# Three-stage chain on one core: the sign of each converted weight as a signed float zero made on GpSimd, the joins a step later, and 26 subtractions moved to GpSimd

## The chip, the cores and the metric

One core of a Trainium2 chip runs the whole program. The metric is the device time of one execution in microseconds (us), lower is better. The engines are called by their names and by the short names of the profile: TensorE (PE, its weight loads PEld), VectorE (DVE), ScalarE (ACT), GpSimd (POOL) and SyncE (SP), whose queue issues nearly all of the transfers.

## The reference

The inputs are of double width in memory where they are weights. What is computed, cut to what matters:

```python
def _attn_ref(q, k, v, tau):            # B, N, C = 2, 6016, 256
    qn = q / (norm(q, axis=1) + 1e-06); kn = k / (norm(k, axis=1) + 1e-06)
    s = kn.transpose(0, 2, 1) @ qn / tau        # 256 x 256 for each batch
    a = softmax(s)
    return v @ a

def _moe_ref(x, w_in, w_out):           # 12032 x 256, 256 x 2048, 2048 x 256
    h = x @ w_in
    return (h - tanh(h)) @ w_out

def _moe2_ref(x, w_gate, w_val, w_out): # 256 x 1536 twice, 1536 x 256
    return (sigmoid(x @ w_gate) * (x @ w_val)) @ w_out
```

The weights `w_in`, `w_out`, `w_gate`, `w_val` and the second `w_out` are stored as 64-bit floats, so the kernel reads each of them as two 32-bit words.

## The kernel before, in words

The columns of `v` (12032 over both batches) are cut into 24 blocks of 496 or 512. Every block goes through `h` (2048 rows, 16 pieces `f` of 128), the elementwise part of the first stage (`emit_E`), `x` (`emit_X`), then the gate and the value (`emit_GV`, 12 pieces), and the output (`emit_O`). The attention matrix of a batch is multiplied into `w_in` once (`aw_chunk`, eight chunks), so that `h` comes straight out of `v`. Nearly every matmul is done in three parts: a number is split into a high part in the fast 32-bit format (a ScalarE copy, `hi`) and a low part (a VectorE subtraction, `lo`), and high times high, high times low and low times high are summed.

The order is written out by hand: a loop over steps `T`, from -4 on, emits for each step, in this order on every engine: the two elementwise halves of the piece whose `h` was computed one step before, the splits for `x` and the output, the gate and value matmuls of the step, the `h` matmuls (ahead of the rest in the first 16 steps), a chunk of `aw` in the even steps up to 12, the `x` matmuls of two steps before, and then the background work. Background work is a list of generators (`running`, filled by `at(step, fn)`): each advances by one `yield` in a step, the older ones first, and those of the same step start after them. An engine runs its instructions in that order and none other.

The weights are converted in the first 250 us, in `conv` (L117 to L150). A generator of `conv` loads a tile of raw words `st` (512 KB, SP's queue), then in the next step ScalarE makes `bt` from the high words (a scaled copy, L135) and a second scaled copy as a half float in place of the high words' upper halves (L136), VectorE puts three bits of the low word beside it (L138) and joins both into the 32-bit float (L143). For the weights of the last two products one more step makes `hi` on ScalarE (L149) and `lo` on VectorE (L150). In the background list `whole` runs a generator, passing over each `yield 1`. In `tail`, in the softmax of the first batch, every `yield` counts, and a list written by hand places them. There are 34 conversions: eight of `w_in` (`conv_win`), eight of the first `w_out` (`conv_w1`, into `w1_f`, split later by `split_w1`, L184 and L187) and 18 of the second stage (`conv_m2`).

The raw tiles of the last 28 of them come from the pool `v4`, which has three buffers and also holds the loaded blocks of `v` (`load_v`) and the output tiles. Between step 4, where block 1 of `v` is loaded, and step 16, where it is split, one of the three is taken. `conv_w1` of chunk 2 to 7 starts at the steps 3, 5, ... 13, and `conv_m2` at 4, 6, ... 14 and then by a formula that keeps it ahead of `GV0`, the steps of the first block's gate matmuls.

GpSimd does a few memsets at the start, and from step 54 on one sum of squares every second step (L688, `acc`). PSUM has four buffers for `h`, `aw`, gate and value.

Of the kernel before, what the change touches and what calls it, by code (L numbers as in the profile page):

```python
# [8 lines left out]
F32 = mybir.dt.float32  # L9
F32R = mybir.dt.float32r  # L10
BF16 = mybir.dt.bfloat16
U32 = mybir.dt.uint32
U16 = mybir.dt.uint16
F16 = mybir.dt.float16
AF = mybir.ActivationFunctionType
ALU = mybir.AluOpType
AX = mybir.AxisListType

P = 128
# [8 lines left out]
def kernel(  # L28
# [13 lines left out]
    nc = tc.nc  # L42
# [18 lines left out]
    rest, i = N - WB * nb, nb // 2  # L61
    assert 0 <= rest <= nb * (TB - WB)
    while rest:
        widths[i] += QB
        rest -= QB
        i = (i + 1) % nb
    blocks = []
    for b in range(B):
        t = 0
# [6 lines left out]
    const = ctx.enter_context(tc.tile_pool(name="const", bufs=1))  # L76
# [16 lines left out]
    def cv(name, shape=(P, 512)):  # L93
        return cv_p.tile(list(shape), F32, tag="cv", name=name)
# [4 lines left out]
    def psw(name, shape=(P, 512)):  # L99
        return ps_w.tile(list(shape), F32, tag="w", name=name)  # L100

    ones = const.tile([P, P], F32, name="ones")
    nc.vector.memset(ones, 1.0)
    ident = const.tile([P, P], F32, name="ident")
# [12 lines left out]
    w1_hi = [wp.tile([P, 2, C], F32R, name=f"w1h{i}") for i in range(N1 // 2)]  # L117
    w1_lo = {}
    win_d = dr_p.tile([N1 // 2, P, NK, 2 * P], F32, name="win_d")

    def conv(src, shape, pool, tag, name, w=None, hi=None, lo=None):

        a, m = shape
        st = pool.tile([P, a, 2 * m], U32, tag=tag, name=f"st_{name}")
        nc.sync.dma_start(out=st, in_=src)
        yield
        words = st.rearrange("p a (m t) -> p a m t", t=2)
        low, high = words[:, :, :, 0], words[:, :, :, 1]
        half = st.bitcast(U16).rearrange("p a (m t) -> p a m t", t=4)
        bt = cv(f"cb_{name}", (P, a, m))  # L130
        bu = bt.bitcast(U32)

        nc.scalar.activation(bt, high.bitcast(F32), AF.Copy, scale=2.0**-112)  # L135
        nc.scalar.activation(half[:, :, :, 3].bitcast(F16), high.bitcast(F32), AF.Copy, scale=2.0**-96)  # L136
        yield 1
        nc.vector.tensor_scalar(half[:, :, :, 2], half[:, :, :, 1], 13, None, ALU.logical_shift_right)  # L138
        yield 1
        yield 1  # L140
        if callable(w):
            w = w()
        nc.vector.scalar_tensor_tensor(  # L143
            out=bu if w is None else w.bitcast(U32), in0=bu, scalar=3, in1=high,
            op0=ALU.logical_shift_left, op1=ALU.bitwise_or
        )
        if w is None:
            yield
            nc.scalar.activation(hi, bt, AF.Copy)  # L149
            nc.vector.tensor_tensor(out=lo, in0=bt, in1=hi.bitcast(F32), op=ALU.subtract)  # L150

    def whole(g):

        for x in g:
            if x is None:
                yield

    def words(ap):
        return ap.bitcast(U32)

    def conv_win(i, pool, tag="st"):
        src = words(w_in)[:, i * 512:(i + 1) * 512].rearrange("(k p) f -> p k f", p=P)
        yield from conv(src, (NK, 2 * P), pool, tag, f"wi{i}", w=win[i])
# [7 lines left out]
    w1_f = {}  # L171

    def conv_w1(i):
        src = words(w_out)[i * 256:(i + 1) * 256, :].rearrange("(a p) d -> p a d", p=P)

        def home():
            pool, tag = (wp, f"w1l{i - 4}") if i > 3 else (wp2, f"w2{'hl'[i % 2]}{4 + i // 2}")
            w1_f[i] = pool.tile([P, 2, C], F32, tag=tag, name=f"w1f{i}")
            return w1_f[i]

        return conv(src, (2, C), v4_p, "v4", f"w1{i}", w=home)

    def split_w1(i):
        nc.scalar.activation(w1_hi[i], w1_f[i], AF.Copy)  # L184
        yield
        w1_lo[i] = wp.tile([P, 2, C], F32R, tag=f"w1l{i}", name=f"w1l{i}")
        nc.vector.tensor_tensor(out=w1_lo[i], in0=w1_f[i], in1=w1_hi[i].bitcast(F32), op=ALU.subtract)  # L187


    kq = {}  # L190
# [291 lines left out]
    while len(e_of) < NT:  # L482
        for home in ("x2h", "x2l", *(f"rr{i}" for i in range(6))):
            j = len(e_of)
            n = min(2 if home[0] == "x" else 1, NT - j)
# [174 lines left out]
    def conv_m2(i, which):  # L660
        if which == 2:
            src = words(w_out2)[i * 256:(i + 1) * 256, :].rearrange("(a p) d -> p a d", p=P)
            for x, nm in ((w2_hi, "w2h"), (w2_lo, "w2l")):
                x[i] = wp2.tile([P, 2, 2 * P], F32R, tag=f"{nm}{i}", name=f"{nm}{i}")
            h, lo = w2_hi[i], w2_lo[i]
        else:
            w = (w_gate, w_val)[which]
            src = words(w)[:, i * 512:(i + 1) * 512].rearrange("(k p) f -> p k f", p=P)
            h, lo = ((wg_hi[i], wg_lo[i]), (wv_hi[i], wv_lo[i]))[which]
        return conv(src, (2, 2 * P), v4_p, "v4", f"m{which}{i}", hi=h, lo=lo)  # L670
# [31 lines left out]
    def at(step, fn, *a):  # L702
        bg.setdefault(step, []).append((fn, a))
# [3 lines left out]
    GV0 = (20, 21, 22, 24, 25, 27, 28, 30, 31, 33, 34, 35)  # L707
# [6 lines left out]
    for i in range(N1 // 2):  # L714
        at({6: 16, 2: 18, 7: 19, 3: 20, 4: 21, 5: 23, 0: 25, 1: 26}[i], split_w1, i)
# [4 lines left out]
            at(2 * i - 9 if i < 6 else 2 * i - 5, win_store, i)  # L720
    for n in range(3 * N2 // 2):
        i, w = divmod(n, 3)
        late = GV0[2 * i] - 3 + (w == 2)
        at(min(late, 4 + 2 * n if n < 6 else 7 + 3 * n // 2), lambda i=i, w=w: whole(conv_m2(i, w)))
    at(2 * N1 + 7, ks_load)
    for j in range(NT):
        t = 54 + 2 * j
# [121 lines left out]
```

## Time and profile before

| what | value |
|---|---|
| median of three runs | 2211.99 us (2211.82 to 2213.15) |
| the profiled execution | 2212.01 us, of which the span of the profile is 2210.2 us |
| TensorE busy | 2199.5 us of the span |
| VectorE busy | 1772.7 us |
| ScalarE busy | 1602.0 us |
| GpSimd busy | 66.5 us |
| granted TensorE clock | full in every slice |

The profile is of one execution. An engine's busy time says how much of the span it worked; the waits say what ended its idle time; the tables by stretch of time show where an engine is near its limit. A busy TensorE is not TensorE at its peak, since the ends of its matmuls are modelled. Times that lie outside the span (1.8 us here) are launch and end.

### The profile page before, as it was taken

Reading aid. Unit: us, or ns where it says so; the run is one execution under the profiler, and the core shown is the slowest. Engines: PE = TensorE matmul, PEld = TensorE weight load, DVE = VectorE, ACT = ScalarE, POOL = GpSimd, SP = SyncE. Lnnn points to the kernel's source line nnn. Section 1 sums busy time; section 2 is a strip of 40 time slices with the busy share of each in tenths; the row PEclk is TensorE's granted clock in tenths of the full one; section 3 lists DMA queues with packets and bytes.
Section 4 is the critical chain, followed back from the end, with each engine's and each line's share of the span. In section 5 each row is a group of like instructions: output and inputs, shape, how many; then the busy total and the mean of one; then the engine's idle time right before and its main releaser. Section 6 shows DMA issues by size and latency. Waiting matters only on the chain.

```text
span 2210.2 us, 28820 instructions
## 1 busy us (share of the span) xinstructions
PE 2199.5 (100%) x10338; PEld 1944.1 (88%) x10338; DVE 1772.7 (80%) x2723; ACT 1602.0 (72%) x2811; POOL 66.5 (3%) x53
## 2 busy tenths in 40 slices
PE   9999999999999999999999999999999999999999
PEld 8778899898888888888999999999988888888898
DVE  7889877888888888878787787787787877877773
ACT  7988867777777777767677676776776776767763
POOL 0000000111111110000000000000000000000000
PEclk9999999999999999999999999999999999999999
DMA  9742101111111010001000000000000000000000
GB/s 354 241 147 96 38 1 53 34 29 52 35 29 48 27 36 20 1 24 34 19 19 1 19 19 1 19 19 1 19 20 1 19 20 1 20 1 19 10 1 19
DMA packets 54000, 86.54 MB, mean 39 GB/s; under 512 B 4960, under 2 KB 31072, under 8 KB 53856
## 3 DMA queue, kind: packets, MB, share of 16 engines
q1 hardware_dynamic: 53280, 83.91, 11.6%
q8 instruction: 81, 1.33, 0.3%
q10 hardware_dynamic: 576, 0.79, 0.1%
q14 instruction: 63, 0.52, 0.1%
HBM read 69.73 MB, written 14.94 MB: 38 GB/s over the span
## 4 chain that ended last, share of the span: by engine, by line
PE 93%; DVE 3%; ACT 3%; issue 1%; DMA 1%; ACTq 0%; DVEq 0%
PE o L445 16%; PE h L332 14%; PE h L334 7%; PE x L381 7%; PE x L378 7%; PE x L379 7%; PE va L414 5%; PE va L416 5%; PE va L413 5%; PE ga L414 5%; PE ga L413 5%; PE ga L416 5%; PE x L373 2%; PE kqe L517 1%; PE aw L285 1%
## 5 line engine op out<-in xcount | busy, mean ns | idle before, releaser
L347 DVE SCALAR_TENSOR_TENSOR w<-u,h 128x496 f32<-128x496 f32 (+1 forms) x384 | 259.6, 676 | 228.6 <-ACT t L343 227.7
L350 DVE COPY_PREDICATED w<-m,t 128x496 f32<-128x496 uint16 (+1 forms) x384 | 303.9, 792 | 39.9 <-ACT sr L687 0.5
L342 ACT ACTIVATE u<-h 128x496 f32<-128x496 f32 (+1 forms) x384 | 222.7, 580 | 138.8 <-PE h L334 138.3
L345 ACT ACTIVATE s<-u,cb 128x496 f32<-128x496 f32 (+1 forms) x384 | 273.8, 713 | 0.3 <-DVE w L349 0.3
L346 ACT ACTIVATE m<-u,ct 128x496 bf16<-128x496 f32 (+1 forms) x384 | 272.5, 710 | 0.0
L348 DVE TENSOR_TENSOR t<-h,t 128x496 f32<-128x496 f32 (+1 forms) x384 | 258.4, 673 | 0.0
L349 DVE SCALAR_TENSOR_TENSOR w<-s,w 128x496 f32<-128x496 f32 (+1 forms) x384 | 257.6, 671 | 0.0
L332 PE MATMUL h<-vTh,awh 128*128 128x496 f32 (+1 forms) x768 | 232.8, 385 | 0.0
L334 PE MATMUL h<-vTh,awl 128*128 128x496 f32 (+1 forms) x768 | 225.1, 375 | 0.2 <-DVE awl L291 0.2
L332 PE MATMUL h<-vTl,awh 128*128 128x496 f32 (+1 forms) x768 | 225.0, 375 | 0.0
L343 ACT ACTIVATE t<-h 128x496 f32<-128x496 f32 (+1 forms) x384 | 223.1, 581 | 0.0
L414 PE MATMUL va<-x2h,wvl 128*128 128x496 f32 (+1 forms) x552 | 206.9, 375 | 0.0
L414 PE MATMUL ga<-x2h,wgl 128*128 128x496 f32 (+1 forms) x552 | 206.9, 375 | 0.0
L413 PE MATMUL va<-x2h,wvh 128*128 128x496 f32 (+1 forms) x552 | 206.9, 375 | 0.0
L413 PE MATMUL ga<-x2h,wgh 128*128 128x496 f32 (+1 forms) x552 | 206.8, 375 | 0.0
L425 DVE TENSOR_TENSOR sg<-va,sg 128x496 f32<-128x496 f32 (+1 forms) x288 | 192.2, 667 | 18.1 <-PE va L416 18.1
L424 ACT ACTIVATE sg<-ga 128x496 f32<-128x496 f32 (+1 forms) x288 | 168.6, 585 | 11.2 <-PE ga L416 11.1
L416 PE MATMUL ga<-x2l,wgh 128*128 128x496 f32 (+1 forms) x576 | 168.8, 375 | 0.0
L416 PE MATMUL va<-x2l,wvh 128*128 128x496 f32 (+1 forms) x576 | 168.8, 375 | 0.0
L332 PEld LDWEIGHTS h<-vTh,awh 128*128 128x128 f32 x768 | 144.4, 189 | 24.5 <-issue 6.8
L334 PEld LDWEIGHTS h<-vTh,awl 128*128 128x128 f32 x768 | 145.1, 189 | 17.7 <-DVE awl L291 0.6
L332 PEld LDWEIGHTS h<-vTl,awh 128*128 128x128 f32 x768 | 145.1, 189 | 17.2
(358 smaller groups left out, 4425.8 us busy)
## 6 DMA issues: line engine op xcount, KB each, us to landing
v<-in_v_dram SPq DMA_DIRECT2D x16, 496.0 KB, 4.2
out_dram<-ob SPq DMA_DIRECT2D x15, 496.0 KB, 3.0
sr<-in_q_dram SPq DMA_DIRECT2D x47, 128.0 KB, 2.1
sr<-in_k_dram SPq DMA_DIRECT2D x47, 128.0 KB, 2.3
raw<-in_q_dram SPq DMA_DIRECT2D x13, 384.0 KB, 8.1
raw<-in_k_dram SPq DMA_DIRECT2D x12, 384.0 KB, 8.2
st_wi<-in_moe_w_in_dram SPq DMA_DIRECT2D x8, 512.0 KB, 7.0
st_w<-in_moe_w_out_dram SPq DMA_DIRECT2D x8, 512.0 KB, 4.7
```

Source lines behind the costliest of these rows:

```text
L332: MM(o[:, :n], aw_hi[i][:, kk, fs], turned(p, x[:, kk, :n]), start=x is h and kk == 0, stop=False)
L334: MM(o[:, :n], aw_lo[i][:, kk, fs], turned(p, h[:, kk, :n]), start=False, stop=kk == 1)
L345: nc.scalar.activation(s, u, AF.Square, bias=cb)
L346: nc.scalar.activation(m, u, AF.Relu, bias=ct2)
L347: nc.vector.scalar_tensor_tensor(out=w, in0=u, scalar=C2, in1=hp, op0=ALU.mult, op1=ALU.mult)
L348: nc.vector.tensor_tensor(out=t, in0=hp, in1=t, op=ALU.subtract)
L349: nc.vector.scalar_tensor_tensor(out=w, in0=s, scalar=CG, in1=w, op0=ALU.add, op1=ALU.mult)
L350: nc.vector.copy_predicated(w, m.bitcast(U16), t)
L413: MM(o[:, :n], wht[m // 2][:, d, ms], h[d], start=d == 0, stop=False)
L414: MM(o[:, :n], wlt[m // 2][:, d, ms], h[d], start=False, stop=False)
L416: MM(o[:, :n], wht[m // 2][:, d, ms], lo[d], start=False, stop=d == 1)
L445: MM(ops[p][d][:, :n], w[i][:, a, ds[d]], x, start=m == 0 and w is w2_hi and x is ph, stop=m == N2 - 1 and x is pl)
```

## The change

The sign of a converted weight is kept as a signed float zero in the place of the high word: GpSimd multiplies `bt` by a constant of 2 to the power -126, read from a tile of one column. VectorE then joins the shifted low word with that sign in one step, and `bt` with the result in a second one, both one step later than the conversion's step before. ScalarE's second copy (L136) and VectorE's shift on 16-bit words (L138) are gone. The 18 `lo` of `conv` and the eight of `split_w1` are subtracted on GpSimd. The `conv_m2` generators start one step earlier; `conv_w1` and `conv_win` start where they did.

```diff
+    tiny = const.tile([P, 1, 1], F32, name="tiny")
+    nc.vector.memset(tiny, 2.0**-126)
...
         words = st.rearrange("p a (m t) -> p a m t", t=2)
         low, high = words[:, :, :, 0], words[:, :, :, 1]
-        half = st.bitcast(U16).rearrange("p a (m t) -> p a m t", t=4)
...
         nc.scalar.activation(bt, high.bitcast(F32), AF.Copy, scale=2.0**-112)
-        nc.scalar.activation(half[:, :, :, 3].bitcast(F16), high.bitcast(F32), AF.Copy, scale=2.0**-96)
+        nc.gpsimd.tensor_tensor(
+            out=high.bitcast(F32), in0=bt, in1=tiny.to_broadcast([P, a, m]), op=ALU.mult
+        )
         yield 1
-        nc.vector.tensor_scalar(half[:, :, :, 2], half[:, :, :, 1], 13, None, ALU.logical_shift_right)
-        yield 1
+        yield
+        nc.vector.scalar_tensor_tensor(
+            out=low, in0=low, scalar=29, in1=high, op0=ALU.logical_shift_right, op1=ALU.bitwise_or
+        )
         yield 1
         if callable(w):
             w = w()
         nc.vector.scalar_tensor_tensor(
-            out=bu if w is None else w.bitcast(U32), in0=bu, scalar=3, in1=high,
+            out=bu if w is None else w.bitcast(U32), in0=bu, scalar=3, in1=low,
             op0=ALU.logical_shift_left, op1=ALU.bitwise_or
         )
         if w is None:
             yield
             nc.scalar.activation(hi, bt, AF.Copy)
-            nc.vector.tensor_tensor(out=lo, in0=bt, in1=hi.bitcast(F32), op=ALU.subtract)
+            nc.gpsimd.tensor_tensor(out=lo, in0=bt, in1=hi.bitcast(F32), op=ALU.subtract)
...
-        nc.vector.tensor_tensor(out=w1_lo[i], in0=w1_f[i], in1=w1_hi[i].bitcast(F32), op=ALU.subtract)
+        nc.gpsimd.tensor_tensor(out=w1_lo[i], in0=w1_f[i], in1=w1_hi[i].bitcast(F32), op=ALU.subtract)
...
-        late = GV0[2 * i] - 3 + (w == 2)
-        at(min(late, 4 + 2 * n if n < 6 else 7 + 3 * n // 2), lambda i=i, w=w: whole(conv_m2(i, w)))
+        late = GV0[2 * i] - 4 + (w == 2)
+        at(min(late, 3 + 2 * n if n < 6 else 6 + 3 * n // 2), lambda i=i, w=w: whole(conv_m2(i, w)))
```

## Rows read from the trace of the kernel before

**Rows 1.** The page, part 1: busy us, share of the span, instructions.

```profile
PE 2199.5 (100%) x10338; PEld 1944.1 (88%) x10338; DVE 1772.7 (80%) x2723; ACT 1602.0 (72%) x2811; POOL 66.5 (3%) x53
```

**Rows 2.** Busy time by stretch: us, PE, PEld, DVE, ACT, POOL, clock, DMA.

```profile
75.00:150.00 75.00, 75.00 (x292) 55.20 (x292) 65.71 (x103) 67.60 (x104) 0.00 (x0) 1.00 0.56 175
150.00:200.00 50.00, 50.00 (x225) 42.34 (x225) 44.65 (x73) 44.49 (x75) 0.00 (x0) 1.00 0.37 117
200.00:250.00 50.00, 47.94 (x223) 41.18 (x222) 48.10 (x78) 44.93 (x77) 0.00 (x0) 1.00 0.15 47
```

**Rows 3.** Timeline of TensorE, 200 to 250 us: the lines with a wait.

```profile
227.64 0.49 PE L378 MATMUL x<-g_14h,w1h 128*128 128x496 f32 x1 [0.58 <-ACT g_14h L355]
240.28 0.48 PE L414 MATMUL va<-x2aT,wvl 128*128 128x496 f32 x1 [1.46 <-DVE wvl L150]
```

**Rows 4.** Tiles of the conversion and a memset: durations in ns min/median/max, or mean.

```profile
L135 ACT ACTIVATE cb_m<-st_m x18: 657/670/695, 82.7 to 237.8; 128x512 f32<-128x512 f32 x18
L143 DVE SCALAR_TENSOR_TENSOR cb_m<-cb_m,st_m x18: 691/693/694, 85.6 to 240.9; 128x512 uint32<-128x512 uint32 x18
...
L535 DVE MEMSET ct<- 128x1 f32 x1 | 0.1, 59 | 0.0
```

**Rows 5.** Busy VectorE of L138, L150, L187: sums over 75 to 250 us.

```profile
sum 175.00, DVE 18.73; mean DVE 6.24
...
sum 175.00, DVE 12.24; mean DVE 4.08
...
sum 175.00, DVE 5.45; mean DVE 1.82
```

**Rows 6.** Groups by line and form, 360 to 860 us: busy us, mean ns.

```profile
L688 POOL TENSOR_TENSOR acc<-acc,sr 128x512 f32<-128x512 f32 x46 | 64.4, 1401 | 790.9 <-ACT sr L687 790.9
...
L350 DVE COPY_PREDICATED w<-m,t 128x512 f32<-128x512 uint16 x50 | 49.8, 995 | 5.2
L350 DVE COPY_PREDICATED w<-m,t 128x496 f32<-128x496 uint16 x42 | 41.4, 986 | 4.7 <-ACT sr L687 0.5
...
L356 DVE TENSOR_TENSOR g_7l<-w,g_7h 128x496 fp32r<-128x496 f32 x3 | 2.8, 948 | 0.4
```

**Rows 7.** Timeline of GpSimd and VectorE, 398 to 413 us: start us, us.

```profile
398.99 1.27 POOL L688 TENSOR_TENSOR acc<-acc,sr 128x512 f32<-128x512 f32 x1 [9.26 <-ACT sr L687]
399.12 1.72 DVE L350 COPY_PREDICATED w<-m,t 128x496 f32<-128x496 uint16 x1
...
402.46 0.67 DVE L347 SCALAR_TENSOR_TENSOR w<-u,h 128x496 f32<-128x496 f32 x1 [0.27 <-ACT t L343]
...
404.40 0.73 DVE L350 COPY_PREDICATED w<-m,t 128x496 f32<-128x496 uint16 x1
...
405.82 0.68 DVE L356 TENSOR_TENSOR g_14l<-w,g_14h 128x496 fp32r<-128x496 f32 x1
...
410.52 1.63 POOL L688 TENSOR_TENSOR acc<-acc,sr 128x512 f32<-128x512 f32 x1 [10.26 <-ACT sr L687]
410.94 0.66 DVE L425 TENSOR_TENSOR sg<-va,sg 128x496 f32<-128x496 f32 x1
...
411.73 0.95 DVE L356 TENSOR_TENSOR g_15l<-w,g_15h 128x496 fp32r<-128x496 f32 x1
```

**Rows 8.** Timeline of TensorE, 86 to 98 us: two even steps begin.

```profile
86.68 0.97 PE L332 MATMUL h<-vTh,awh 128*128 128x496 f32 x2
...
88.32 1.89 PE L285 MATMUL aw<-win,aT 128*128 128x256 f32 x8
...
96.83 0.97 PE L332 MATMUL h<-vTh,awh 128*128 128x496 f32 x2
```

**Rows 9.** Tile st_w (raw words of w_out): its loads, issue to landing.

```profile
DMA to landing us min/median/max: 3.1/4.7/7.5
```

**Rows 10.** Timeline of the first softmax, 50 to 54 us.

```profile
50.97 1.35 ACT L136 ACTIVATE st_wi<-st_wi 128x512 f16<-128x512 f32 x1
52.07 0.25 ACT L214 ACTIVATE rn<-n 128x4 f32<-128x4 f32 x1
...
53.20 0.71 PE L236 MATMUL rq<-dg,ones 128*128 128x128 f32 x4 [0.54 <-DVE dg L223]
```

More of the change, by code (lines that the diff above doesn't have):

```diff
@@ L13 @@
 U16 = mybir.dt.uint16
-F16 = mybir.dt.float16
 AF = mybir.ActivationFunctionType
```

## The prediction

> **What bounds the kernel now.** I read the page's first part, and there TensorE: it is busy for 2199.5 of 2210.2 us [rows 1]. All its idle time in the whole span is 10.7 us, so no change to other engines' work can gain more than that, and 0.2% of the time, about what a measurement can tell from no change, is 4.4 us. Next I read the table by stretch for the 250 us in which weights are converted, since the change touches nothing later. The reader is to see two things there [rows 2]. TensorE stands still only in the last stretch, 2.06 us. And VectorE and ScalarE are nearly full: VectorE 65.71 of 75, 44.65 of 50, and 48.10 of 50 us (96.2%) just where TensorE waits. The third view, TensorE's waits in order of time, says what for [rows 3]: 0.58 us for a split that stood behind a late VectorE product, and 1.46 us for the low half `wvl`, the end of VectorE's queue in that step. So the stage is bound by TensorE with VectorE close behind it, and a change here is worth what it does to VectorE's queue. A loss in this stage is not won back, for TensorE is full afterwards.
>
> **ScalarE.** L136 goes, 34 times 1.35 us [rows 10], 46 us. ScalarE is not what TensorE waits for, except that splits stand behind it, so this alone gains little. At one place it is on the path: in the first softmax the square root `rn` starts at 52.07 behind an L136 that began at 50.97, and TensorE then idles 0.54 us for the product that follows [rows 10]. I take 0.5 us for it; the ends are 0 (another step of that chain comes next) and 0.54.
>
> **VectorE's own work.** Over 75 to 250 us it loses L138, 18.73 us, and the subtractions L150 and L187, 12.24 and 5.45 us [rows 5]. It gains a first join for each conversion. At 0.75 us apiece, 18.73 us are 25 conversions; a join of the new form (two 32-bit operands in SBUF, 512 columns, shift and or) is the old join's operation with another shift, 0.693 us [rows 4], so 25 of them are 17.3 us. Before, VectorE was busy for 65.71 + 44.65 + 48.10 = 158.5 us of these 175 [rows 2]; after, 158.5 - 36.4 + 17.3 = 139.4 us, if nothing disturbs it.
>
> **GpSimd's work, and what it does to VectorE.** GpSimd is idle in this stage [rows 2]. It gets 25 products and 26 subtractions in it, 51 operations of two 32-bit tensors of 512 columns. The nearest row is the sum L688 with 1.27 us when nothing is in its way [rows 7]. The product writes every second word and reads a constant of stride zero, which no row shows; I take 1.3 us for it, between 1.27 and the 1.63 of a disturbed sum. GpSimd's own load, 51 times 1.3 us or 66 of 175, is no bound, and the joins wait a step for the product. The price lies elsewhere. At 398.99 a sum starts on GpSimd; the predicated copy that VectorE begins at 399.12 takes 1.72 us, where the same copy takes 0.73 at 404.40. At 410.52 the sum starts while a copy runs, and takes 1.63; VectorE's L425, which reads PSUM, runs beside it in its usual 0.66, and L356, both of whose operands are in SBUF, takes 0.95 in place of 0.68 [rows 7]. So a GpSimd operation and a VectorE operation on two SBUF tensors exclude each other, and whichever comes second waits.
>
> The Trainium skill says it as a rule, GPSIMD Engine Reference, Key points: GpSimd shares its SBUF interfaces with VectorE, in contention with VectorE's instructions that have two SBUF inputs or run in a two-port mode. The trace agrees for two inputs (1.72 against 0.73 us). By the two-port half, which no row here shows, the small operations after `rn` would wait for the product of the conversion beside them, and the 0.5 us of the softmax would be nothing.
>
> What one operation costs VectorE: between 360 and 860 us, 92 predicated copies took 0.995 and 0.986 us in the mean [rows 6] against 0.73 [rows 7], 0.26 more, 24 us in all; and seven groups of three subtractions like the last row took 0.95 against 0.68 [rows 6, 7], 5.7 us. That is 29.7 us for 46 sums, 0.64 us each. The bounds are 0 (VectorE waits for something else, or reads PSUM) and 0.99 (the longest of these rows, 1.72 less 0.73). I take 0.64, since that is the mean over a stage with the same elementwise work; the joins added here are of the kind that is hit. 51 times 0.64 is 32.6 us, so VectorE has 139.4 + 32.6 = 172.0 us to do. It kept up to 96.2% at best, with TensorE already waiting, so it needs 172.0 / 0.962 = 178.8 us for what now takes 175: 3.8 us lost. The 2.06 us of waiting are inside these 175 and so not to be added.
>
> **The steps that move.** Both conversions of a pair now start at the same odd step (3, 5, ... 13), and the joins of both come two steps later, in the same step as the next pair's loads. Of `v4`'s three buffers the block of `v` holds one from step 4 to 16, so those loads wait on SP's queue for those joins, which before were a step ahead; behind them on that queue stand the loads of q and k, which have a rotation of buffers to spare. Behind the loads ScalarE's L135 waits, and behind that the whole next step on ScalarE. The round: the first load lands 4.7 us after its buffer is free [rows 9]; the second goes out two joins later, 1.4 us; L135 takes 0.67 [rows 4]; then an activation of about that length, from L347 to the end of the copy 2.67 us (402.46 to 405.13) [rows 7], the low half of `aw` 0.68, and two joins, 1.4: 12.2 us by durations. VectorE's neighbours overlap by 0.09 us, so 11.5 is the lower end. A pair of steps lasts 96.83 - 86.68 = 10.15 us [rows 8]. So each pair falls 1.35 to 2.05 us back, four pairs 5.4 to 8.2. The slack: `h` is done at 88.3, the low half of `aw` could be made by 88.3 + 0.67 + 2.67 + 0.68 = 92.3 and is needed at 96.83 [rows 8], 4.5 us. What is left, 0.9 to 3.7 us, is late for TensorE. I take 1.5, near the lower end, because part of it is the same idle time that the sum for VectorE has used.
>
> **At no cost.** `tiny` is one memset of 0.06 us [rows 4] ahead of the warm-up matmuls; what follows those waits for loaded data, and without that cover it would cost its 0.06. In the loading of the first batch six products and six joins come and six L138 go; they run beside loads that set the pace there, and each would cost at most a product's 1.3 us. The subtractions' latency (1.27 against 0.68) costs nothing as long as GpSimd starts them right behind `hi`; they leave the end of VectorE's queue, so `wvl` should come earlier than it did.
>
> **The sum.** 3.8 + 1.5 - 0.5 = 4.8 us more than the profiled execution's 2212.01, which stands 0.02 above the median: 2216.8 us.
>
> **The rivals.**
> First, on the other side: GpSimd's operations fall where VectorE waits for ScalarE or reads PSUM. Then VectorE really is relieved, and the waits of rows 3 (2.04 us) and the 0.5 go: 2209.5 us. It decides below 0.53 us for an operation: 139.4 + 51 x 0.53 = 166.4, 96.2% of the 172.9 us that TensorE works. For it: ScalarE, freed of 46 us, runs ahead, and half of the elementwise operations read PSUM. Against: the mean of 0.64 was measured with such operations present.
> Second, exclusion at a price near the long row: at 0.8 us VectorE has 180.2 us, needs 187.3, and loses 12.3; with 1.5 and -0.5 that is 2225.3 us; at 0.99 it would be 2235. For it: joins and splits make VectorE's share of two-SBUF work larger here than later, and a product that takes longer than 1.3 us acts the same way. Against: half of the sums met a cheaper place.
> Third, the loads: if they land after 7.5 us instead of 4.7 [rows 9], each pair falls 2.8 more behind, four pairs 11.2, 2228. Against: 7.5 is the longest of eight.
>
> **How the numbers follow.** The forecast, exclusion at 0.64 with some lateness of loads, has 0.50, and its own range is 2213 to 2221. The first rival has 0.27, the second 0.18, the third 0.05. The likeliest time is 2216.8, at the edge of what can be told from no change: of its 0.50 I put 0.23 within 0.2% (up to 2216.4) and 0.27 beyond. Of the first rival 0.03 lie below 2207.6 and 0.24 within. So faster 0.03, same 0.47, slower 0.50. The range reaches from the first rival, 2209, to between the second's two prices, 2230, and leaves out about 0.2.
>
> **What would show it.** Right: in 75 to 250 us copies L350 and joins L143 longer than 0.73 and 0.69 beside GpSimd's work, VectorE near 98% busy, and TensorE's waits for `g`, `p` or `awl` of several us; SP's waits for joins and ScalarE's waits for loads at L135 in 80 to 140 us. The wait for `wvl` is gone or smaller. Wrong: VectorE clearly below 96% with L350 near 0.75 (first rival); GpSimd products of 2 us or more, or copies of 1.5 us in the mean (second). The sum fails first in the 0.64 us, which was measured where sums and copies meet at fixed places.

## The result and the profile after

The changed kernel takes 2228.72 us (median of 4 runs, 2227.58 to 2231.43), the kernel before 2211.90 in the same comparison (4 runs, 2211.28 to 2213.15): a ratio of 1.0078, interval 1.0067 to 1.0090. It is slower by 16.8 us, where 4.8 were forecast. The profiled execution has a span of 2227.2 us, 17.0 more than before.

The page of the changed kernel, part 1, is the first thing to read beside [rows 1].

```profile
PE 2204.8 (99%) x10338; PEld 1944.4 (87%) x10338; DVE 1781.1 (80%) x2698; ACT 1561.6 (70%) x2777; POOL 146.8 (7%) x113
```

ScalarE has 40 us less to do and GpSimd 80 more. VectorE has 8 us more, though 34 shifts and 26 subtractions left it and only 34 joins came. TensorE's idle time grew from 10.7 to 22.4 us, and its busy time by 5.3, for the same matmuls. Part of the 5.3 is the granted clock: it is 0.93 in the mean from 100 to 150 us (the table below), which makes 3.5 us by an estimate.

The table by stretch of the changed kernel, for the stretches of [rows 2] and with two halves of the first one, says where.

```profile
75.00:150.00 75.00, 68.43 (x247) 47.85 (x245) 53.46 (x77) 41.81 (x75) 20.54 (x18) 0.95 0.43 142
150.00:200.00 50.00, 48.82 (x204) 38.48 (x205) 46.46 (x63) 37.34 (x67) 22.85 (x17) 1.00 0.45 143
200.00:250.00 50.00, 45.97 (x215) 39.96 (x214) 48.08 (x63) 36.47 (x66) 19.73 (x15) 1.00 0.24 73
...
100.00:125.00 25.00, 22.06 (x78) 14.99 (x76) 16.84 (x25) 12.70 (x23) 6.70 (x6) 0.93 0.46 158
125.00:150.00 25.00, 21.96 (x76) 15.37 (x76) 18.02 (x27) 13.55 (x25) 6.77 (x6) 0.93 0.32 106
```

Two different losses stand here. From 200 to 250 us VectorE works 48.08 of 50 us (96.2%, as before) and TensorE waits 4.03 us in place of 2.06. From 75 to 150 us TensorE waits 6.57 us in place of none, and there VectorE works 53.46 of 75 us and ScalarE 41.81, both far less than before. A stage in which every engine has room waits for something else. (From about 160 us on the same work lies 14 us later than before, so the later stretches don't hold quite the same steps as those of [rows 2].)

TensorE's waits from 75 to 330 us in the changed kernel, by what ended them (us in total, times, longest):

```profile
PE h L335 <- ACT awh L293: 4.7, 3, 2.1
...
PE x L381 <- ACT g_14h L358: 2.1, 1, 2.1
PE x L381 <- ACT g_11h L358: 1.9, 1, 1.9
PE h L337 <- DVE awl L294: 1.5, 3, 0.5
PE x L376 <- DVE w1f L146: 1.2, 1, 1.2
...
PE va L417 <- POOL wvl L153: 0.8, 1, 0.8
```

`awh`, `awl` and `w1f` belong to the steps 8 to 18, `g` and `wvl` to the steps 29 to 33. To put us on each I took from TensorE's timelines the start of the first `h` matmul of every step and subtracted that of the kernel before. The lag at four steps, for the changed kernel and the experiments below (one profiled execution each):

| kernel | T=7 | T=18 | T=28 | T=34 |
|---|---|---|---|---|
| after | 0.06 | 13.96 | 13.97 | 17.20 |
| e2 steps alone | 0.28 | 19.38 | 19.87 | 18.98 |
| e3 even steps | -1.05 | 5.62 | 6.53 | 9.21 |
| e1 free buffers | -0.27 | -0.27 | 0.66 | 3.35 |
| e7 three buffers | -0.60 | -0.60 | -0.57 | 3.39 |
| e5 products alone | -0.85 | -0.66 | -0.27 | 1.73 |
| e4 subtractions alone | -0.58 | -0.58 | 0.50 | 3.42 |
| e6 zero on ScalarE | -1.51 | -1.51 | -1.51 | -2.44 |
| e9 negative bias, early | -1.76 | -1.76 | -1.77 | -3.73 |
| e10 early alone | -0.52 | -0.52 | -0.52 | -1.39 |
| e11 products first | -0.66 | -0.60 | 1.11 | 0.23 |

Of the 17.2 us, 13.9 arise in the steps 8 to 18 and 3.2 in the steps 29 to 34; behind that the lag stays. The column T=7 is read with care: e10 differs from the kernel before only later and is 0.52 ahead there, and the changed kernel, e1, e3 and e7, which do the same up to step 1, are 1.1 us apart already at step 1.

**The first loss** is a loop. This is the timeline of the changed kernel for one round of it, from the joins to the next joins:

```profile
100.47 0.38 SPq L126 DMA_DIRECT2D st_w<-in_moe_w_out_dram  x1
...
101.80 0.38 SPq L126 DMA_DIRECT2D st_m<-in_moe_w_out_dram  x1
...
104.73 0.67 ACT L134 ACTIVATE cb_w<-st_w 128x512 f32<-128x512 f32 x1 [2.33 <-DMA st_w<-in_moe_w_out_dram]
...
107.45 0.66 ACT L134 ACTIVATE cb_m<-st_m 128x512 f32<-128x512 f32 x1 [2.04 <-DMA st_m<-in_moe_w_out_dram]
...
108.02 0.57 ACT L345 ACTIVATE u<-h 128x496 f32<-128x496 f32 x1
...
109.09 0.67 DVE L350 SCALAR_TENSOR_TENSOR w<-u,h 128x496 f32<-128x496 f32 x1 [4.00 <-ACT t L346]
...
110.79 0.69 PE L335 MATMUL h<-vTh,awh 128*128 128x496 f32 x2 [2.07 <-ACT awh L293]
...
111.65 0.67 DVE L294 TENSOR_TENSOR awl<-aw,awh 128x512 fp32r<-128x512 f32 x1
112.25 0.68 DVE L140 SCALAR_TENSOR_TENSOR st_w<-st_w 128x512 uint32<-128x512 uint32 x1
...
113.72 0.38 SPq L126 DMA_DIRECT2D st_w<-in_moe_w_out_dram  x1
```

The loads go out when the joins free the buffers, ScalarE stands before the landed data, the elementwise step stands behind ScalarE, and the next joins behind the elementwise step on VectorE. No instruction of TensorE is a link of it: `u` at 108.02 starts right behind `cb_m`, without a wait, and so do those of the other rounds (94.76, 120.91, 134.17). The first loads of the rounds go out at 88.08, 100.47, 113.72, 126.62 and 139.87: rounds of 12.39, 13.25, 12.90 and 13.25 us, where a pair of steps takes TensorE 10.15 [rows 8].

SP's waits in the changed kernel say the same from the other end:

```profile
SPq L126 <- DVE w1f L146: 45.8, 6, 10.4
...
SPq L126 <- DVE cb_m L146: 32.7, 10, 11.8
```

Before they were 9.2 and 19.8 us. Such a wait is no loss by itself: e7 below still has 28.8 and 29.0 us of them and no first loss.

**The second loss** is one place in step 29 and one in step 32. Timeline of GpSimd, VectorE, ScalarE and TensorE at the first:

```profile
222.84 0.66 DVE L350 SCALAR_TENSOR_TENSOR w<-u,h 128x496 f32<-128x496 f32 x1
...
223.61 1.27 POOL L153 TENSOR_TENSOR wvl<-cb_m,wvh 128x512 fp32r<-128x512 f32 x1 [2.41 <-ACT wvh L152]
...
224.01 1.40 DVE L352 SCALAR_TENSOR_TENSOR w<-s,w 128x496 f32<-128x496 f32 x1
224.84 1.47 POOL L135 TENSOR_TENSOR st_m<-cb_m,tiny 128x512 f32<-128x512 f32 x1
225.51 1.36 DVE L353 COPY_PREDICATED w<-m,t 128x496 f32<-128x496 uint16 x1
...
226.91 0.62 ACT L358 ACTIVATE g_11h<-w 128x496 fp32r<-128x496 f32 x1 [2.32 <-DVE w L353]
...
227.58 0.50 PE L381 MATMUL x<-g_11h,w1h 128*128 128x496 f32 x1 [1.88 <-ACT g_11h L358]
```

A subtraction and a product on GpSimd meet the two VectorE operations whose operands all lie in SBUF, one behind the other. Each takes 0.6 to 0.7 us longer. VectorE is late already when the step begins. In the kernel before, L350's counterpart starts here:

```profile
207.88 0.66 DVE L347 SCALAR_TENSOR_TENSOR w<-u,h 128x496 f32<-128x496 f32 x1
```

With the lag of 13.97 us that would be 221.85, and it starts at 222.84, 1.0 us later, behind two joins of the step before that GpSimd had lengthened (1.17 us at 218.90 and 1.65 at 220.10). VectorE has no wait from 191.87 to 229.12 us in which it could catch up; before, it had none from 195.81 to 216.00. So the split comes 2.4 us late, and TensorE waits 1.88 us for it.

### The profile page after: what moved, and what is told of

Its sections match the earlier page's. It is cut to its first block, busy times and chain, and to the rows that moved or that the text cites. A ratio compares the mean times of both kernels' runs of the same rounds, so it can differ in the third digit from the quotient of the medians.

```text
span 2227.2 us, 28910 instructions
## 1 busy us (share of the span) xinstructions
PE 2204.8 (99%) x10338; PEld 1944.4 (87%) x10338; DVE 1781.1 (80%) x2698; ACT 1561.6 (70%) x2777; POOL 146.8 (7%) x113
## 3 DMA queue, kind: packets, MB, share of 16 engines
q1 hardware_dynamic: 53280, 83.91, 11.5%
q8 instruction: 81, 1.33, 0.3%
## 4 chain that ended last, share of the span: by engine, by line
PE 86%; DVE 5%; DMA 4%; ACT 3%; issue 2%; SPq 0%; POOL 0%; ACTq 0%; DVEq 0%
PE o L448 15%; PE h L335 13%; PE x L384 6%; PE h L337 6%; PE x L382 6%; PE x L381 6%; PE va L417 5%; PE va L419 5%; PE va L416 5%; PE ga L416 5%; PE ga L417 5%; PE ga L419 5%; DVE w L353 1%; DVE w L352 1%; DMA st_wi<-in_moe_w_in_dram 1%
## 5 line engine op out<-in xcount | busy, mean ns | idle before, releaser
L350 DVE SCALAR_TENSOR_TENSOR w<-u,h 128x496 f32<-128x496 f32 (+1 forms) x384 | 259.4, 675 | 244.4 <-ACT t L346 243.7
L353 DVE COPY_PREDICATED w<-m,t 128x496 f32<-128x496 uint16 (+1 forms) x384 | 311.7, 812 | 40.3 <-ACT sr L690 0.5
L352 DVE SCALAR_TENSOR_TENSOR w<-s,w 128x496 f32<-128x496 f32 (+1 forms) x384 | 266.2, 693 | 0.0
L351 DVE TENSOR_TENSOR t<-h,t 128x496 f32<-128x496 f32 (+1 forms) x384 | 258.1, 672 | 0.0
```

Source lines behind the costliest of these rows:

```text
L350: nc.vector.scalar_tensor_tensor(out=w, in0=u, scalar=C2, in1=hp, op0=ALU.mult, op1=ALU.mult)
L351: nc.vector.tensor_tensor(out=t, in0=hp, in1=t, op=ALU.subtract)
L352: nc.vector.scalar_tensor_tensor(out=w, in0=s, scalar=CG, in1=w, op0=ALU.add, op1=ALU.mult)
L353: nc.vector.copy_predicated(w, m.bitcast(U16), t)
```

## The experiments

Each time is the median of 4 to 11 runs beside runs of the kernel before, whose medians lay between 2211.65 and 2211.79 us. Two theories were open at first: the loads, bound to the joins, make the loss (the loop above), or exclusion between GpSimd and VectorE makes it.

**e1: buffers freed early.** The changed kernel, with the loads of a pair in two steps again, and `v`'s block 1 loaded at step 13 instead of 4, so that `v4` has all three buffers for raw words.

```diff
-        at(min(late, 3 + 2 * n if n < 6 else 6 + 3 * n // 2), lambda i=i, w=w: whole(conv_m2(i, w)))
+        at(min(late, 4 + 2 * n if n < 6 else 6 + 3 * n // 2), lambda i=i, w=w: whole(conv_m2(i, w)))
...
-        if e0 and e0[1] == (4 if T < N1 else 12) and e0[0] + 1 < NB:
+        if e0 and e0[1] == (13 if T < N1 else 12) and e0[0] + 1 < NB:
```

> The changed kernel, but the first six conversions of the second stage start at the even steps 4 to 14 again, and block 1 of v is loaded at step 13 in place of 4, so that each load finds a buffer that was freed a step before. Theory of the loads (each pair of loads waits for joins of the same step; 13.9 of the 17.0 us that were lost): those 13.9 us go, and about 3 us of loss stay, 2214 to 2216 us. Theory of the exclusion (GpSimd holds VectorE up; the late loads follow from late joins): the loss stays above 10 us, 2222 or more.

Measured: 2215.89 us, ratio 1.0018 (1.0009 to 1.0027). All of GpSimd's work is still there, and the first loss is gone. Its row by stretch:

```profile
75.00:150.00 75.00, 75.00 (x293) 55.21 (x292) 71.93 (x95) 50.75 (x91) 29.52 (x23) 1.00 0.60 182
```

TensorE stands full beside a VectorE of 71.93 us (53.46 in the changed kernel) and 23 GpSimd operations. 4.2 us are left, 3.6 of them in the table: 2.7 are the second loss, and 0.9 arises between the `h` of step 18 and that of step 19, where GpSimd lengthens two joins and the elementwise operation L352 to 1.10, 1.64 and 1.57 us and TensorE waits 0.64 us for `w`.

**e2: the steps alone.** The operations of the kernel before, GpSimd idle, joins and starts a step later and earlier as in the changed kernel.

```diff
         yield 1
+        yield
         nc.vector.tensor_scalar(half[:, :, :, 2], half[:, :, :, 1], 13, None, ALU.logical_shift_right)
         yield 1
-        yield 1
...
-        late = GV0[2 * i] - 3 + (w == 2)
-        at(min(late, 4 + 2 * n if n < 6 else 7 + 3 * n // 2), lambda i=i, w=w: whole(conv_m2(i, w)))
+        late = GV0[2 * i] - 4 + (w == 2)
+        at(min(late, 3 + 2 * n if n < 6 else 6 + 3 * n // 2), lambda i=i, w=w: whole(conv_m2(i, w)))
```

> The kernel before with its own operations and nothing on GpSimd, but with the steps of the changed one: the shift and the join a step later, the conversions of the second stage a step earlier. Theory of the loads: the loss comes without GpSimd too, and a little more per pair, since the half-float copy stands on ScalarE behind the second load: 13 to 20 us slower than before, 2225 to 2232. Theory of the exclusion: within 2 us of before, 2210 to 2214.

Measured: 2230.78 us, 1.0085 (1.0071 to 1.0099). Without one GpSimd operation in the stage the lag at step 18 is 19.4 us, more than in the changed kernel, since each round also holds ScalarE's L136 (rounds of 13.5 to 14.3 us, against 12.4 to 13.25). Its row by stretch:

```profile
75.00:150.00 75.00, 65.85 (x239) 46.37 (x238) 49.34 (x78) 53.15 (x80) 0.00 (x0) 0.95 0.43 139
```

VectorE has a third of its time free while TensorE idles 9.15 us. With e1 this settles the first loss: it needs the moved steps and not GpSimd.

**e3: even steps only.** The first line of e1's edit without the second.

> The changed kernel with only the start of those six conversions put back on even steps; block 1 of v still holds a buffer. Theory of the loads: one load in a step, none 1.3 us behind another, but each still waits for the joins of its own step: most of the loss goes, 2215 to 2220. Theory of the exclusion: 2222 or more, as for the run with free buffers.

Measured: 2221.66 us, 1.0043 (1.0029 to 1.0057), over the bound. Two steps for the loads of a pair cure about half of the first loss (from T=7 to 18 the lag grows by 6.7 us in place of 13.9); a wait of 3.5 us for `w1f` is left in step 16.

**e7: three buffers only.** The second line of e1's edit without the first: both loads of a pair in one step, as in the changed kernel, with a third buffer.

> The changed kernel, only block 1 of v is loaded at step 13 in place of 4; the pairs still start at the same odd steps. Theory of the loads: the first load of a pair finds a free buffer, the second waits for the joins of the first, so the round of 13 us shrinks to 11 to 11.5 and 4 to 7 of the 13.9 us stay: 2218 to 2223. If it is only the two starts in one step that matter (two conversions' work bunched): no gain, 2226 to 2229.

Measured: 2215.55 us, 1.0018 (1.0009 to 1.0027), better than expected and the same as e1. So one buffer decides: with a third one the first load of a pair doesn't wait for the joins of its own step. The two that went out at 100.47 and 101.80 go out at 92.38 and 96.15 here (92.97 and 96.66 before the change), and up to step 28 the lag doesn't grow.

**e4: the subtractions alone.** The kernel before, with its 26 subtractions on GpSimd.

```diff
-            nc.vector.tensor_tensor(out=lo, in0=bt, in1=hi.bitcast(F32), op=ALU.subtract)
+            nc.gpsimd.tensor_tensor(out=lo, in0=bt, in1=hi.bitcast(F32), op=ALU.subtract)
...
-        nc.vector.tensor_tensor(out=w1_lo[i], in0=w1_f[i], in1=w1_hi[i].bitcast(F32), op=ALU.subtract)
+        nc.gpsimd.tensor_tensor(out=w1_lo[i], in0=w1_f[i], in1=w1_hi[i].bitcast(F32), op=ALU.subtract)
```

> The kernel before with only the 26 subtractions moved to GpSimd; signs, steps and loads as before. Theory of the loads: no loss, since no load moves; VectorE sheds 17.7 us: 2209 to 2212. Theory of the exclusion with 0.64 us for each of 26: 16.6 us come back to VectorE, so about as before, 2211 to 2213; with 0.99 us: 8 us on VectorE more than shed, 2215 to 2220.

Measured: 2215.89 us, 1.0019 (1.0010 to 1.0028): the time belongs to the dear price, but the price was not dear. VectorE is busy for 157.48 us from 75 to 250, where 158.5 less the 17.7 of the subtractions [rows 2, 5] would be 140.8: 16.7 us for 26 operations, 0.64 each, just the price forecast. VectorE so has a little less to do than before, and the kernel is 4.2 us slower all the same. Its timeline shows the reason:

```profile
210.22 1.27 POOL L150 TENSOR_TENSOR wvl<-cb_m,wvh 128x512 fp32r<-128x512 f32 x1 [3.26 <-ACT wvh L149]
210.62 1.41 DVE L349 SCALAR_TENSOR_TENSOR w<-s,w 128x496 f32<-128x496 f32 x1
212.13 0.71 DVE L350 COPY_PREDICATED w<-m,t 128x496 f32<-128x496 uint16 x1
...
213.55 0.49 PE L378 MATMUL x<-g_11h,w1h 128*128 128x496 f32 x1 [1.26 <-ACT g_11h L355]
```

The subtraction used to stand at the end of VectorE's queue in the step, where little waits for it. On GpSimd it starts in the middle of the elementwise work, on which TensorE waits a step later. And as in the changed kernel VectorE is late when the step begins, by 1.1 us: L347 starts at 209.46, where 207.88 and the lag of 0.50 make 208.38, behind a shift L138 that waited 0.72 us for ScalarE and then took 1.67 us beside a subtraction.

**e5: the products alone.** e1 with the 26 subtractions back on VectorE.

> As the run with free buffers, but the 26 subtractions are back on VectorE: of the change only the 34 products on GpSimd and the two joins stay. Theory of the exclusion, as priced in the prediction (0.64 us for each GpSimd operation beside VectorE): VectorE has 158.5 - 18.7 + 17.3 + 25 x 0.64 = 173.1 us of work in 175, so 2 to 5 us of loss, 2214 to 2217. If only what GpSimd does right behind the high halves is costly (the subtractions run in the part where the gate matmuls want their halves), the loss goes: 2210 to 2213.

Measured: 2213.31 us, 1.0008 (0.9999 to 1.0017), not told from no change, and between the two ranges, so it decides for neither. VectorE's copies take 0.982 us in the mean here too, so the products alone lengthen them; but VectorE's busy time, 166.59 us, is near that of e1 (167.63), and the time is 2.6 us shorter. Again the busy time doesn't say what a kernel loses.

**e6, e8, e9: the zero on ScalarE.** The kernel before with the sign's zero made by ScalarE in the place of the half float; joins where they were, GpSimd idle. In these three the zero comes out without its sign, with a bias of 0 (e6) and of -0.0 (e8, e9), so negative weights enter as positive ones; the work is the same. e9 starts the later conversions one step earlier.

```diff
...
-        nc.scalar.activation(half[:, :, :, 3].bitcast(F16), high.bitcast(F32), AF.Copy, scale=2.0**-96)
+        nc.scalar.activation(high.bitcast(F32), bt, AF.Copy, scale=2.0**-126)
...
-        nc.vector.tensor_scalar(half[:, :, :, 2], half[:, :, :, 1], 13, None, ALU.logical_shift_right)
+        nc.vector.scalar_tensor_tensor(
+            out=low, in0=low, scalar=29, in1=high, op0=ALU.logical_shift_right, op1=ALU.bitwise_or
+        )
...
```

> The kernel before with the signed float zero made on ScalarE, from bt, in place of the half float, and the two joins on VectorE in the same step as before; nothing on GpSimd and no step moved. The exclusion and the late loads are both absent; ScalarE has a copy of 0.67 us in place of one of 1.35, 34 times, and the square root of the first softmax stands 0.7 us less behind: 2209 to 2211.5 us. If ScalarE's copies cost TensorE nothing even there: as before, 2211.9 within 0.5.

> As the run with the zero made on ScalarE, whose copy adds a bias of plus zero to its product, so that a negative zero would come out without its sign; here the bias is minus zero, and nothing else differs. The work is the same: 2209.1 us within 0.5, 2 to 3 us faster than before. If the bias costs ScalarE something per copy, up to 2211.

> The same, and the last twelve conversions of the second stage start one step earlier, so that their low halves stand a step earlier in VectorE's queue than the gate matmuls that read them. If the 1.5 us for the low half of the value weights is a matter of that queue's order, it goes: 2207 to 2208.5. If VectorE is simply full in that step, something else waits in its place: 2208.5 to 2210.

Measured: e6 2209.11 us, 0.9988 (0.9980 to 0.9997); e8 2209.28, 0.9989 (0.9980 to 0.9998); e9 2208.72, 0.9986 (0.9977 to 0.9995). Without GpSimd and the moved steps a gain is there: 2.5 us, and with the earlier start 3.1. e8's bias of -0.0 did not keep the sign, as it was meant to. e9 lies 0.2 us inside its second range, although in its profile the wait for `wvl` is gone and no wait of TensorE over 0.2 us is left from 75 to 330 us. ScalarE's second copy takes 0.68 us here in place of 1.36, the first join 0.68 in place of L138's 0.75 (medians of `st_m`).

**e10: the earlier start alone.** The kernel before with one edit, which keeps the half float:

```diff
-        late = GV0[2 * i] - 3 + (w == 2)
-        at(min(late, 4 + 2 * n if n < 6 else 7 + 3 * n // 2), lambda i=i, w=w: whole(conv_m2(i, w)))
+        late = GV0[2 * i] - 4 + (w == 2)
+        at(min(late, 4 + 2 * n if n < 6 else 6 + 3 * n // 2), lambda i=i, w=w: whole(conv_m2(i, w)))
```

> The kernel before, unchanged in every operation; only the conversions of the second stage from the seventh on start one step earlier. The step that the wait for `wvl` (1.46 us in the kernel before) comes from a conversion started too late: that wait goes, up to 1.5 us less, 2210.3 to 2211.3. Rival, VectorE's queue being full in these steps (48.10 of 50 us): the conversions only push the same work forward, the wait reappears at a gate matmul, 2211.5 to 2212.5.

Measured: 2210.69 us, 0.9996 (0.9987 to 1.0005). The wait for `wvl` is gone; small waits for `g` appear in its place, and of its 1.46 us 0.87 are won (T=28 to 34). It lies as expected, but can't be told from no change. It is the fastest of the kernels that keep the sign; none of these beats the kernel before by more than can be told.

**e11: products for the first conversions only.** e1's buffers, e10's start, products on GpSimd up to the sixth `conv_m2`, half floats behind it, all subtractions on VectorE.

```diff
+        if pr:
+            nc.gpsimd.tensor_tensor(
+                out=high.bitcast(F32), in0=bt, in1=tiny.to_broadcast([P, a, m]), op=ALU.mult
+            )
...
+        else:
+            nc.scalar.activation(half[:, :, :, 3].bitcast(F16), high.bitcast(F32), AF.Copy, scale=2.0**-96)
...
+        return conv(src, (2, 2 * P), v4_p, "v4", f"m{which}{i}", hi=h, lo=lo, pr=i < 2)
```

> The products on GpSimd for the first conversions only (those of w_in, of w_out and the first six of the second stage); the other twelve keep the half float; all subtractions on VectorE; the free buffers of e1 and the earlier start of e10. If GpSimd's work costs only where the gate matmuls of the first block wait for halves, the 0.85 us that e5 was ahead until step 16 stays, and with e10's gain the time is 2210 to 2211.3. If exclusion costs also in the steps 8 to 18, or the clock falls after some wait there, the time is 2212 to 2214.

Measured: 2212.67 us, 1.0004 (0.9995 to 1.0013). The time fell into the second branch for a reason that neither named. Its timeline where it loses 1.7 us, at the end of step 18, the place where e1 loses 0.9:

```profile
146.88 1.35 ACT L149 ACTIVATE st_m<-st_m 128x512 f16<-128x512 f32 x1
...
147.98 0.66 ACT L355 ACTIVATE u<-h 128x496 f32<-128x496 f32 x1
...
151.99 0.72 DVE L363 COPY_PREDICATED w<-m,t 128x496 f32<-128x496 uint16 x1
...
152.76 1.93 PE L386 MATMUL x<-w,w1f 128*128 128x496 f32 x4 [1.43 <-DVE w L363]
```

No GpSimd operation runs there and every one has its usual length: the low halves of the last conversion with a product (`w2l`) and of the first with a half float (`wgl`) fall into one step, with `w1l`, a shift and a join (five operations from 146.87 to 150.06), and `w`, behind them on VectorE, is late.

## Why the prediction was right in its sign and too small

**The steps that move** is the step that failed: "What is left, 0.9 to 3.7 us, is late for TensorE. I take 1.5". The mechanism was the one described, and it measured 13.9 us. Two numbers in it were off. That the time still lies inside the stated range, 2209 to 2230, is luck: its upper end was drawn for the second rival's price, which is not there, and the forecast's own range, 2213 to 2221, was missed by 7.7 us.

The round was 12.4 to 13.25 us, not 11.5 to 12.2. By the timeline above, the second load is used 5.65 us after its issue, where 4.7 of [rows 9] was taken (six loads of q and k go out on the same queue in that time; whether they make it late was not tested); and ScalarE makes `u` and `t` behind the load before VectorE can begin, 1.07 us and not one activation of 0.67. The rest held: 1.33 to the second issue (1.4), 2.56 from L350 to the end of the copy (2.67), 1.47 for two joins (1.4); with 0.57 for L134 and 0.60 for the low half of `aw` these make the 13.25 us of this round. The four rounds fall back 11.2 us (51.79 less four times 10.15), where 5.4 to 8.2 were reckoned.

The slack of 4.5 us was not there. It was counted from the end of the `h` matmuls at 88.3, as if ScalarE could begin at once; but the first pair of late loads went out only at 88.08, and already this round held the low half of `aw` back. It started at 98.40, where the slack's sum put its end at 92.3. The sum also took the wrong matmul: the line at 96.83 in [rows 8] reads the high half `awh`, and the kernel before reads the low half first at 98.06. The remaining 2.7 of the 13.9 us I did not divide further; the wait of 1.2 for `w1f` at the end of the loop is in it. The third rival gave 2228, near the result, with this mechanism and another cause: the loads of `st_w` landed after 3.9 us in the median. That it came near is luck too.

**GpSimd's price** came out near its number: 3.8 us were forecast, 3.2 are lost in the steps 29 to 34, and e1 and e7, without the first loss, are 4.2 and 3.9 slower than before. Two things blur this. In the same steps e10 and e2, without GpSimd, gain 0.9 us from the earlier start, so GpSimd costs the changed kernel 4.1 there. And part of the loss of e1 and e7 is a lower clock behind a wait, which the changed kernel does not have in these steps (the last section). The rate was 0.64 at most. Groups by line and form, 75 to 265 us, of the changed kernel (busy us, mean ns):

```profile
L353 DVE COPY_PREDICATED w<-m,t 128x496 f32<-128x496 uint16 x31 | 30.7, 992 | 3.2
L352 DVE SCALAR_TENSOR_TENSOR w<-s,w 128x496 f32<-128x496 f32 x31 | 29.5, 952 | 0.0
L351 DVE TENSOR_TENSOR t<-h,t 128x496 f32<-128x496 f32 x31 | 20.7, 666 | 0.0
...
L146 DVE SCALAR_TENSOR_TENSOR cb_m<-cb_m,st_m 128x512 uint32<-128x512 uint32 x18 | 15.3, 851 | 0.6
L140 DVE SCALAR_TENSOR_TENSOR st_m<-st_m 128x512 uint32<-128x512 uint32 x18 | 14.2, 791 | 0.0
```

and the same operations in e2, where GpSimd is idle:

```profile
L350 DVE COPY_PREDICATED w<-m,t 128x496 f32<-128x496 uint16 x32 | 23.2, 725 | 3.3
L349 DVE SCALAR_TENSOR_TENSOR w<-s,w 128x496 f32<-128x496 f32 x31 | 20.7, 666 | 0.0
```

The copies grew from 725 to 992 ns, L352 from 666 to 952, the joins from about 690 to 851 and 791; L351, which reads PSUM, stays at 666. That is 8.3 + 8.9 + 2.9 + 1.9 = 22 us, 0.43 for each of the 51 GpSimd operations in this stretch (four single operations that are longer as well add 2.4 us, which makes 0.48); by busy time it is 0.55 in e1 ((167.6 - 139.4) / 51) and 0.64 in e4, so the second rival's 0.8 is not there. This is the exclusion of [rows 7].

How the sum made a loss from it was not right, though. It filled VectorE over 175 us and took what overflowed 96.2%. By that e4, with VectorE less busy than before, would lose nothing, and e5 nearly as much as e1. The loss comes in two steps, where VectorE is behind already and GpSimd's operation falls on the elementwise chain that TensorE waits for next. Nor was VectorE 98% busy over the 175 us, as the prediction's signs had it: 148.0 us (85%), since the loop held it up, and 167.6 (96%) in e1. The other signs came: longer copies and joins, TensorE's waits for `g` and `awl` (none for `p`), SP's for joins and ScalarE's for loads. The agreement of 3.8 with 3.2 is partly luck.

**The first rival** named 0.53 us as the point below which VectorE is relieved. The rate was 0.43 to 0.48 in the changed kernel, which still lost 3.2 us in the steps 29 to 34: the point was worked out from the same total and falls with it.

**The softmax.** The 0.5 us were not won. Timeline of the changed kernel beside [rows 10]:

```profile
51.51 1.62 POOL L135 TENSOR_TENSOR st_wi<-cb_wi,tiny 128x512 f32<-128x512 f32 x1 [1.91 <-ACT rn L217]
52.14 1.01 DVE L221 TENSOR_SCALAR rn<-rn 128x4 f32<-128x4 f32 x1
...
53.74 0.71 PE L239 MATMUL rq<-dg,ones 128*128 128x128 f32 x4 [0.92 <-DVE dg L226]
```

and of e6, without GpSimd:

```profile
50.97 0.17 DVE L219 TENSOR_SCALAR rn<-rn 128x4 f32<-128x4 f32 x1
...
52.03 0.61 PE L237 MATMUL rq<-dg,ones 128*128 128x128 f32 x4
```

An operation on four columns takes 1.01 us beside the product and 0.17 alone. It has one tensor in SBUF, so the two-input half of the rule doesn't cover it. The Trainium skill (GPSIMD Engine Reference, Key points) also names VectorE's two-port mode as a case of contention; this row agrees with that half, which the kernel before did not show, though no row names the mode. A second row agrees: in e4 the shift L138, on one tensor, takes 1.67 us at 205.91 beside a subtraction, and 0.75 in the median. The wait for `dg` is 0.92 us after and 0.27 in e5, with the product; without it 0.54 before, none in e4, 0.2 in e10 and 0.8 in e2, whose operations here are those of before. So the term is nothing, within what executions differ by.

**At no cost** held where it was put: GpSimd's own load is no bound, the wait for `wvl` fell from 1.46 to 0.76 us, and the products took 1.04 us in the median where 1.3 was taken.

## What to carry to other kernels

When a load moves behind the operation that frees its buffer in an in-order queue, write the whole round from one free buffer to the next, with every instruction that stands between on each engine, and set its first round, not an idle engine, against the slack; a third buffer was worth 13 us here. Work given to GpSimd is priced by the VectorE operations that it meets on the way to what TensorE waits for next, and by how far VectorE is behind there, not by VectorE's total over a stage: read which two-SBUF operations run in that step and the one before, and who waits for them. A stage that loses while all its engines have room can be a loop of transfers: look at the issuing queue's waits, and take one buffer more as the test.

## What had not been expected of the hardware

TensorE's clock falls behind some short waits. Table by stretch of e1's TensorE (us, busy, clock, DMA), around its wait of 1.90 us for `g_11h`:

```profile
212.00:214.00 2.00, 0.38 (x2) 1.00 0.88 236
214.00:216.00 2.00, 1.71 (x5) 0.72 0.45 149
216.00:218.00 2.00, 2.00 (x6) 0.50 0.00 0
218.00:220.00 2.00, 2.00 (x10) 0.93 0.00 0
```

The granted clock goes from 1.00 to 0.50, which is 1.2 in place of 2.4 GHz, and comes back; the lag grows by 3.8 us in this step for a wait of 1.9. The changed kernel has nearly the same wait (1.88 us at 227.58) and a clock of 1.00 behind it:

```profile
226.00:228.00 2.00, 0.42 (x2) 1.00 0.94 262
228.00:230.00 2.00, 2.00 (x11) 1.00 0.07 25
```

There the lag grows by 2.1. In e7 the same two waits, for `g_11h` (1.9 us) and `g_14h` (2.1), leave the clock at 1.00 behind the first and at 0.50 from 232 to 234 us behind the second. So a wait can cost its length or twice that. The Trainium skill (TensorE: Matmul & The Clock Gate, HAM oscillation) describes a kernel whose clock falls again at every wait for its loads; the rows agree that it falls, and here it does not at each wait. What decides between these two was not tested. In the steps 8 to 18 of the changed kernel the clock also falls (the mean of 0.93 from 100 to 150 us above), and from 96 to 166 us TensorE is idle for only 7.75 of the 13.9 us that it falls back; the rest it is counted as busy, at the lower clock or around its waits. But the loop there has no link on TensorE, so by that reading the clock adds nothing to the loop: at full speed TensorE would have waited in its place. No run tested this.

A product of 512 columns with a constant of stride zero, written to every second word, takes 1.04 us on GpSimd, less than the 1.27 of a sum of two tensors. And a product that underflows keeps no sign on ScalarE, with a bias of 0 (e6) or of -0.0 (e8), while GpSimd's does (the changed kernel).
